# A two-layer spectral and feed-forward kernel: first stage rebuilt, folds moved to the vector engine, sums moved into matmuls, and a new instruction order

## The chip, the cores and the metric

The kernel runs on one core of a Trainium2 chip. The metric is device time in microseconds (us), the median of several executions. The engines are named as in the profile: PE (matmul), DVE (vector), ACT (scalar, here mostly copies out of PSUM), POOL (GpSimd), SP (issues DMAs).

## The reference, cut to what matters

```python
def _A_ref(x, w_r, w_i):                      # x: 1 x 2048 x 448
    X = rfft2(x) * (w_r + 1j * w_i)           # two-dimensional real FFT, pointwise filter
    return irfft2(X)
def _B_ref(x, w1, b1, w2, b2):                # 448 -> 1792 -> 448
    h = relu(x @ w1 + b1) ** 2
    return h @ w2 + b2
x = x + _A_ref(layernorm(x)); x = x + _B_ref(layernorm(x))
x = x + _A_ref(layernorm(x)); x = x + _B_ref(layernorm(x))
```

The Fourier transforms are matmuls with constant tables. A layer passes through these stages, and the text uses their names: **A** (first factor along the 2048 rows), **TD** (along the 448 columns), **B** (second factor along the rows), **W** (the filter, on DVE), **Bi, TI, AI** (the inverse of B, TD, A), then LayerNorm and the two dense matmuls. The stretch from TI to the first dense matmuls is called the ramp. A fold is the sum and the difference of two halves; a mirror is a row of the filter W read backwards. A row tile is 128 x 448, and there are 16.

## The kernel before

Instructions are recorded with their reads and writes, then a list scheduler fixes the order on every engine before anything runs. A unit with a higher `bias` goes first among those that are ready in the scheduler's model. At run time an engine takes its instructions in that order, as ACT does in the trace: its square root at 12.68 us (below) has its input from 10.04 us on, but stands behind an eviction, for which ACT waits idle for 0.47 us.

The first stage, per tile: DVE makes the statistics, ACT the square root, DVE the reciprocal and a 128 x 128 tile `Ms` of -2 x mean, POOL the scaled table `Fs`; PE runs five matmuls of 256 columns; ACT evicts.

```python
def first_A(t, evac):
    f, m = Fs[:, t % 4, :], Ms[:, t % 4, :]
    ts(f, FA_sb[:], rstd[:, t, 0:1], 1.0, ALU.mult, ALU.mult, eng="pool")
    ts(m, ones[:], mv[:, t, 0:1], -2.0, ALU.mult, ALU.mult)
    stage_A(t, x_sb[:, t, 0:D], xr[:, t, :], f, m, evac)
def w_direct():                               # six copies on POOL: rows of W to their places
    for a, b in ((0, 3), (3, 7)):
        cp(Wp[:, a:b, 0, 0:225], Wn[:, 0, a + 1:b + 1, :], eng="pool")
        ...
def w_mirror(p):                              # reversed rows of W by matmul, evicted by ACT
    ...
    act(Wp[:, p - 1, 1:4:2, 0:225], q[...])
def stage_W(p0, n):                           # the filter for the pairs p0 .. p0+n-1
    ...
    tt(T[6], T[3], T[2], ALU.subtract)
    tt(T[7], T[4], T[5], ALU.add)
    tt(z[:, :, 0], T[6][:, :, 1], T[6][:, :, 0], ALU.subtract)      # four folds
    tt(z[:, :, 3], T[6][:, :, 1], T[6][:, :, 0], ALU.add)
    tt(z[:, :, 1], T[7][:, :, 0], T[7][:, :, 1], ALU.subtract)
    tt(z[:, :, 2], T[7][:, :, 0], T[7][:, :, 1], ALU.add)
def second_A(t):                              # first stage of the second layer: 4 x 256 columns
    y = yA[:, t % 8, :]
    for h in range(2):
        ts(y[:, HD * h:HD * (h + 1)], x_sb[:, t, 0:HD] if h == 0 else x_sb[:, t, D - 1:HD - 1:-1],
           mv[:, t, 0:1], rstd[:, t, 0:1], ALU.subtract, ALU.mult)
    stage_A(t, y[:, 0:HD], y[:, HD:D], FA_sb[:], None, "act")
```

Of the kernel before, what the change touches and what calls it, by code (L numbers as in the profile page):

```python
# [19 lines left out]
EPS = 1e-5  # L20

# [9 lines left out]
def make_constants():  # L31
# [61 lines left out]
    return dict(FA=np.concatenate([FA, -FA], 1), FI=np.concatenate([FI, -FI], 1), TD=TD, G=G, H=H, TI=TI,  # L93
                J=np.eye(P)[::-1])


class _Op:
    __slots__ = ("eng", "fn", "deps", "has_dep", "ticket", "is_dma", "dsem", "cost", "lat", "unit", "gdeps")

    def __init__(self, eng, fn, is_dma, cost, lat):  # L100
        self.eng = eng
        self.fn = fn
        self.deps = []
        self.gdeps = []
        self.has_dep = False
        self.ticket = None
        self.is_dma = is_dma
        self.dsem = None
        self.cost = cost
        self.lat = lat  # L110
        self.unit = None

# [46 lines left out]
def _pages(ap):  # L159

    if isinstance(ap, _PsAP):
        return [ap.tile]
    pat = list(ap.ap)
    row = pat[0][0]
    name = ap.tensor.name
    off = np.array([ap.offset % row if row else ap.offset])
    for step, cnt in pat[1:]:
        off = (off[:, None] + step * np.arange(cnt)[None, :]).reshape(-1)
    pg = np.unique(off * mybir.dt.size(ap.dtype) // 8)
    return [(name, int(i)) for i in pg]  # L170


class _Sched:
# [6 lines left out]
    DMA_RATE = 280.0  # L180

    def __init__(self):
# [4 lines left out]
        self.bias = 0.0  # L187

# [39 lines left out]
    def schedule(self):  # L228
# [24 lines left out]
        free = {e: 0.0 for e in self.ENGINES}  # L253
        done = {}
# [4 lines left out]
        dma_free = 0.0  # L259
        for u in self.units:  # L260
            if left[u] == 0:
                cand[u.eng].append(u)
# [26 lines left out]
        while total:  # L289
            choice = None  # L290
            for e in self.ENGINES:
                best = None
                avail = {}
                for u in cand[e]:
# [7 lines left out]
                    start = max(r, free[e])  # L302
                    key = (start, -u.prio, u.seq)
                    if best is None or key < best[0]:
                        best = (key, u)
                if best is not None and (choice is None or best[0] < choice[0]):
                    choice = best
            assert choice is not None, "no unit can run"
            start, u = choice[0][0], choice[1]
            e = u.eng  # L310
            cand[e].remove(u)
# [12 lines left out]
            for op in u.ops:  # L324
# [3 lines left out]
                if op.is_dma:  # L328
                    dma_free = max(dma_free, t) + op.lat
                    done[op] = dma_free + 1800.0  # L330
                for a in (op.gdeps if e != "pe" else ()):
                    if a.eng == "pe" and a.unit.tile is not None:
                        for i in range(a.unit.tile.bank, a.unit.tile.bank + a.unit.tile.n):
                            bank_free[i] = max(bank_free[i], t + op.lat)
            free[e] = t
            for v in order[u]:
                left[v] -= 1
                if left[v] == 0:
                    cand[v.eng].append(v)
        self.length = max(done.values())  # L340
        for e in self.ENGINES:
# [33 lines left out]
def bass_interleave_layers__spectral_gfnet__dense_activation_squared_relu__prompt_kernel(nc, A_x, A_w_r, A_w_i, B_x, B_w1, B_b1, B_w2, B_b2, out):  # L375
# [6 lines left out]
    with ExitStack() as es:  # L382
# [7 lines left out]
        x_sb = sb("x_sb", [P, NT, 4 * P])  # L390
        XA = sb("XA", [P, 2, 2, 16, P])
# [12 lines left out]
        Wn = yT[:].rearrange("p a b c -> p (a b c)")[:, 0:2 * 16 * 225].rearrange("p (r k l) -> p r k l", r=2, k=16)  # L404
# [3 lines left out]
        H_sb = sb("H_sb", [P, 9, 2, 2 * P])  # L408
# [5 lines left out]
        Ms = sb("Ms", [P, 4, P])  # L414
# [3 lines left out]
        c_rem = sb("c_rem", [P, FF], FP32)  # L418
# [56 lines left out]

        def tt(o, a, b, op, eng="dve"):
# [19 lines left out]

        x_dram = A_x.rearrange("b (p t) d -> p (b t) d", t=NT)
# [7 lines left out]
        for a, b in pieces:  # L505
            dma("sp", x_sb[:, a:b, 0:D], x_dram[:, a:b, :])
        memset(ones[:], 1.0, eng="pool")
        memset(x_sb[:, :, D:4 * P], 0.0, eng="pool")
        memset(Wt[:, :, 224:226], 0.0, eng="pool")
        memset(W1_sb[64:128, 3, :], 0.0)  # L510
        for a, b in pieces:
            cp(xr[:, a:b, :], x_sb[:, a:b, D - 1:HD - 1:-1], eng="pool")

        for i, w in enumerate((A_w_r, A_w_i)):
            dma("sp", Wn[:, i, :, :], w.rearrange("(p k) l -> p k l", k=16))
        dma("sp", J_sb[:], dc["J"])
        dma("sp", G_sb[:, 2:9], dc["G"][:, 2:9])
        dma("sp", H_sb[:, 2:9], dc["H"][:, 2:9])
        dma("sp", G_sb[:, 0:2], dc["G"][:, 0:2])
        dma("sp", H_sb[:, 0:2], dc["H"][:, 0:2])  # L520
        dma("sp", TI_sb[:], dc["TI"])
# [6 lines left out]
        def w1_aux():  # L528

            qs = []  # L530
            for i in range(4):
# [6 lines left out]
                act(c_rem[64:97, f], q[lambda b: ps[64:97, b, 0:D]], ACT.Copy, scale=-1.0 / D)  # L538
            for r in (65, 67):
                dma("sp", W1_sb[r:r + 1, 3, :], B_b1.rearrange("(o f) -> o f", o=1))  # L540
            lo, c = W1_sb[96:97, 3, :], c_rem[96:97, :]
            tt(lo, c, lo, ALU.subtract)


        Wp = Wt[:, 0:28, :].rearrange("p (q s) l -> p q s l", s=4)
        W08 = Wt[:, 28:32, :].rearrange("p (q s) l -> p q s l", s=2)

        def w_direct():
            for a, b in ((0, 3), (3, 7)):
                cp(Wp[:, a:b, 0, 0:225], Wn[:, 0, a + 1:b + 1, :], eng="pool")  # L550
                cp(Wp[:, a:b, 2, 0:225], Wn[:, 1, a + 1:b + 1, :], eng="pool")
            for i in range(2):
                cp(W08[:, :, i, 0:225], Wn[:, i, 0:9:8, :], eng="pool")

        def w_mirror(p):

            q = _Tile(1)
            for i in range(2):
                mm(q[lambda b, i=i: ps[:, b, i * LW:i * LW + 225]], J_sb[:], Wn[:, 1 - i, 16 - p, :],
                   i == 0, i == 1, skip=True)  # L560
            act(Wp[:, p - 1, 1:4:2, 0:225],
                q[lambda b: ps[:, b, 0:2 * LW].rearrange("p (r l) -> p r l", r=2)[:, :, 0:225]])


        def ln_stats(ts_):
            for t in ts_:
                small(lambda e, t=t: e.bn_stats(st[:, t, 0:6], x_sb[:, t, 0:D]), [x_sb[:, t, 0:D]], [st[:, t, 0:6]], 540.0)  # L567
                small(lambda e, t=t: e.bn_aggr(mv[:, t, 0:2], st[:, t, 0:6]), [st[:, t, 0:6]], [mv[:, t, 0:2]])  # L568
            a, b = ts_[0], ts_[-1] + 1
            act(mv[:, a:b, 1], mv[:, a:b, 1], ACT.Sqrt, bias=epst[:, 0:1])  # L570

# [8 lines left out]
        def stage_A(t, y, yr, F, M, evac):  # L580
            q = _Tile(1)
            F2 = F[:, None, 0:P].to_broadcast([P, 2, P])
# [4 lines left out]
            for k in range(2):  # L587
                d0 = D0[k]
                mm(o(k), y[:, d0:d0 + P], F2, k == 0, False, skip=True)
                mm(o(k), yr[:, d0:d0 + P], F, False, k == 1 and M is None, skip=True)  # L590
            if M is not None:
                mm(q[lambda b: ps[:, b, :].rearrange("p (k g c) -> p k g c", k=2, g=2)[:, :, 0, :]], M, F2,
                   False, True, skip=True)
            src = q[lambda b: ps[:, b, :].rearrange("p (k c j) -> p k c j", k=4, c=16)]
            dst = XA[:, :, :, :, 8 * t:8 * t + 8].rearrange("p k g c j -> p (k g) c j")
            if evac == "act":
                act(dst, src)
            else:
                cp(dst, src)

        def first_A(t, evac):

            f, m = Fs[:, t % 4, :], Ms[:, t % 4, :]
            ts(f, FA_sb[:], rstd[:, t, 0:1], 1.0, ALU.mult, ALU.mult, eng="pool")
            ts(m, ones[:], mv[:, t, 0:1], -2.0, ALU.mult, ALU.mult)
            stage_A(t, x_sb[:, t, 0:D], xr[:, t, :], f, m, evac)


        def stage_TD(p):
            q = _Tile(2)  # L610
# [5 lines left out]
            act(U[:, 2 * p:2 * p + 2, :], q[lambda b: ps[:, b:b + 2, 0:2 * LW]])  # L616

        def stage_B(p):
            q = _Tile(2)
# [18 lines left out]
            act(EF[:, 2 * p:2 * p + 2, :], q[lambda b: ps[:, b:b + 2, 0:2 * LW]])  # L638

        def stage_W(p0, n):  # L640

            if p0 > 0:
# [10 lines left out]
                tt(T[5], T[1], wa, ALU.mult)  # L653
                tt(T[6], T[3], T[2], ALU.subtract)
                tt(T[7], T[4], T[5], ALU.add)
                z = Z[:, 4 * p0:4 * (p0 + n), :].rearrange("p (q s) l -> p q s l", s=4)
# [16 lines left out]
        def stage_Bi(p):  # L673
            q = [_Tile(1), _Tile(1)]
            if p > 0:
                i = p + 1
                z = Z[:, 4 * p:4 * p + 4, :]
                for lb in range(2):
                    for g in range(2):
# [3 lines left out]
                    act(VT[:, lb, :, :, 2 * p:2 * p + 2, :],  # L683
                        q[lb][lambda b: ps[:, b, :].rearrange("p (g t c j) -> p g t c j", g=2, t=16, c=2)])
            else:
                z = Z[:, 0:4, :].rearrange("p (q s) l -> p q s l", s=2)
                for lb in range(2):
# [4 lines left out]
                    for c in range(2):  # L692
                        act(VT[:, lb, :, :, c, :],
                            q[lb][lambda b, c=c: ps[:, b, c * 256:(c + 1) * 256].rearrange(
                                "p (g t j) -> p g t j", g=2, t=16)])


        def stage_TI(t, n):
# [6 lines left out]
            act(TIo[:, t:t + n, :, :], q[lambda b: ps[:, b:b + n, 0:D].rearrange("p i (g d) -> p i g d", g=2)])  # L705

        def stage_AI(t, n):
# [14 lines left out]
            for i in range(n):  # L722
                xx = x_sb[:, t + i, 0:D].rearrange("p (h d) -> p h d", h=2)
                r = q[lambda b, i=i: all_.f(b)[:, :, i, :]]
                small(lambda e, xx=xx, r=r, i=i: e.scalar_tensor_tensor(  # L725
                    out=xx, in0=_res(r), scalar=1.0, in1=xx, op0=ALU.mult, op1=ALU.add, accum_out=sd[:, t + i, 0:1]),
                    [r, xx], [xx, sd[:, t + i, 0:1]], 600.0)
# [3 lines left out]
        def ln_B(t, n):  # L731
# [17 lines left out]
            sch.bias -= 30000.0  # L749
# [3 lines left out]
            sch.bias += 30000.0  # L753
# [23 lines left out]
        def second_A(t):  # L777
            y = yA[:, t % 8, :]
            for h in range(2):
                ts(y[:, HD * h:HD * (h + 1)], x_sb[:, t, 0:HD] if h == 0 else x_sb[:, t, D - 1:HD - 1:-1],  # L780
                   mv[:, t, 0:1], rstd[:, t, 0:1], ALU.subtract, ALU.mult)
            stage_A(t, y[:, 0:HD], y[:, HD:D], FA_sb[:], None, "act")
# [3 lines left out]
        def spectral(first):  # L786
            items = (1, 2, 3, 4, 5, 6, 7, 0)
# [124 lines left out]
```

## Time and profile before

| | before |
|---|---|
| time, median | 311.0 us (309.89 to 311.18) |
| span of the profiled execution | 310.7 us |
| first TD matmul (end of the first stage) | 25.32 us |
| first TI matmul of layer 1 (end of the first spectral part) | 54.03 us |
| last tile's addition in layer 1 | 166.48 us |
| first TD of layer 2 | 170.44 us |
| first TI of layer 2 | 199.42 us |
| last tile's addition in layer 2 | 307.49 us |

The marks are starts of instructions in the timeline. The differences between them give stages that tile the span exactly. The page's first part has the busy time of each engine, its share of the span and the number of instructions:

```profile
PE 279.3 (90%) x1710; PEld 166.4 (54%) x1710; DVE 192.7 (62%) x606; ACT 181.8 (58%) x381; POOL 17.3 (6%) x34
```

Ninety per cent is an average over unlike stages. The view by windows shows one stage alone; its columns are the window, its length, busy us and instructions of PE, PEld, DVE, ACT and POOL, the granted clock, the DMA share and GB/s:

```profile
30.00:40.00 10.00, 9.23 (x78) 7.02 (x77) 9.86 (x27) 10.00 (x18) 0.00 (x0) 1.00 0.00 1
40.00:50.00 10.00, 8.67 (x58) 5.16 (x56) 9.72 (x22) 9.93 (x19) 0.00 (x0) 1.00 0.01 2
```

In the first spectral part DVE and ACT are both saturated, and PE waits for them. The first stage looks different. In PE's timeline (start, length, engine, line, operation, what was written from what, and in brackets the idle time before and what ended it):

```profile
7.72 0.37 PE L455 MATMUL ps<-Fs,x_sb 128*128 128x256 bf16 x1 [7.72 <-POOL Fs L487]
7.89 0.42 PE L455 MATMUL ps<-Fs,VT 128*128 128x256 bf16 x1
...
20.10 0.27 PE L455 MATMUL ps<-Fs,x_sb 128*128 128x256 bf16 x1
20.21 0.27 PE L455 MATMUL ps<-Fs,VT 128*128 128x256 bf16 x1
...
25.32 1.74 PE L455 MATMUL ps<-TD_sb,XA 128*128 128x226 bf16 x16 [0.88 <-ACT XA L474]
```

The lengths overlap (the first ends at 8.09 us, the second starts at 7.89), so the step from one start to the next is what counts. It is about 0.21 us for 256 columns at the beginning and 0.109 us after 19.9 us: half rate first, full rate later. Meanwhile ACT's timeline has a square root (`mv`) right behind evictions (`XA`) that wait for those slow matmuls,

```profile
12.18 0.60 ACT L474 ACTIVATE XA<-ps 128x512 bf16<-128x512 f32 x1 [0.47 <-PE ps L455]
12.68 0.29 ACT L474 ACTIVATE mv<-mv,epst 128x2 f32<-128x2 f32 x1
```

and DVE's timeline shows who waits for the square root:

```profile
9.96 0.59 DVE L567 BATCH_NORM_STATS2 st<-x_sb 128x6 f32<-128x448 bf16 x1
13.00 0.17 DVE L575 RECIPROCAL rstd<-mv 128x2 f32<-128x2 f32 x1 [2.45 <-ACT mv L474]
13.08 0.40 DVE L487 TENSOR_SCALAR Ms<-ones,mv 128x128 bf16<-128x128 bf16 x2
```

DVE, whose statistics every later step of the stage needs, stands idle for 2.45 us, because ACT's queue has the eviction first. The group of the `Ms` operations (count, then busy us in all, mean ns of one, idle us before them):

```profile
L487 DVE TENSOR_SCALAR Ms<-ones,mv 128x128 bf16<-128x128 bf16 x16 | 3.2, 242 | 0.0
```

And the end of layer 1 in PE's timeline:

```profile
162.76 1.04 PE L455 MATMUL ps<-FA_sb,tmp 128*128 128x256 bf16 x8
...
170.44 3.98 PE L455 MATMUL ps<-TD_sb,XA 128*128 128x226 bf16 x24 [0.69 <-ACT XA L474]
...
177.50 2.54 PE L455 MATMUL ps<-TD_sb,XA 128*128 128x226 bf16 x24 [0.25 <-ACT arena L474]
```

After a wait for the last tile 24 TD matmuls take 3.98 us at 170.44, and the next 24, seven us later, take 2.54 us: PE had dropped to half rate again.

### The profile page before, as it was taken

The numbers are of one execution on the slowest core, as the hardware profiler recorded it, in microseconds if no ns is written. First come the engines' busy times: TensorE is split into PE (matmuls) and PEld (weight loads), VectorE is DVE, ScalarE is ACT, GpSimd is POOL, SyncE is SP. The second block draws the span as 40 slices with busy tenths as digits, with TensorE's granted clock in tenths as the row PEclk, the third lists the DMA queues.
The fourth block names the chain that finished last, engine by engine and source line by source line (L and its number), as shares of the span: only waits on it lengthen the run. The fifth ranks groups of instructions, "written<-read, shape, count | busy, mean of one in ns | idle before, by whom it ended". The sixth has DMA issues, their size and how long they took to land.

```text
span 310.7 us, 4816 instructions
## 1 busy us (share of the span) xinstructions
PE 279.3 (90%) x1710; PEld 166.4 (54%) x1710; DVE 192.7 (62%) x606; ACT 181.8 (58%) x381; POOL 17.3 (6%) x34
## 2 busy tenths in 40 slices
PE   0798997989999999999996987787999999999995
PEld 0566664758554554555453664555854454454452
DVE  5661997898575476596465399498624443473431
ACT  2468999899246427735713688698804623651620
POOL 4655000000000000000000000000000000000000
PEclk9999999999999999999999899999999999999999
DMA  7997000074000000030000000016000020013001
GB/s 225 420 394 214 1 2 1 10 107 89 2 1 2 0 0 3 0 62 8 0 0 0 2 1 0 2 34 127 12 31 32 0 63 32 0 33 96 0 15 44
DMA packets 25435, 16.03 MB, mean 52 GB/s; under 512 B 17666, under 2 KB 24322, under 8 KB 25412
## 3 DMA queue, kind: packets, MB, share of 16 engines
q1 hardware_dynamic: 25124, 15.44, 17.8%
q10 hardware_dynamic: 288, 0.30, 0.3%
q8 instruction: 13, 0.21, 0.3%
q14 instruction: 10, 0.08, 0.1%
HBM read 9.70 MB, written 1.84 MB: 37 GB/s over the span
## 4 chain that ended last, share of the span: by engine, by line
PE 72%; ACT 11%; DVE 10%; issue 3%; DMA 1%; POOL 1%; SPq 0%; DVEq 0%; POOLq 0%
PE ps L455 72%; DVE tmp L478 5%; ACT arena L474 4%; ACT VT L474 3%; DVE x_sb L725 2%; DVE arena L478 2%; ACT sq_out L733 1%; DMA x_sb<-in_A_x_dram 1%; ACT XA L474 1%; ACT Wt L474 1%; DVE st L567 1%; POOL Fs L487 1%; DVE x_sb L773 0%; ACT sd L474 0%; ACT tmp L474 0%
## 5 line engine op out<-in xcount | busy, mean ns | idle before, releaser
L474 ACT ACTIVATE arena<-ps 128x512 bf16<-128x512 f32 (+2 forms) x172 | 99.0, 598 | 55.8 <-PE ps L455 53.8
L455 PE MATMUL ps<-yT,W_sb 128*128 128x512 bf16 (+1 forms) x560 | 99.7, 337 | 2.8 <-ACT arena L474 2.5
L455 PE MATMUL ps<-W_sb,arena 128*128 128x448 bf16 x448 | 87.0, 352 | 0.0
L455 PEld LDWEIGHTS ps<-yT,W_sb 128*128 128x128 bf16 x560 | 54.1, 98 | 46.3 <-ACT arena L474 4.4
L478 DVE TENSOR_TENSOR arena<-arena 128x512 bf16<-128x512 bf16 (+1 forms) x140 | 51.8, 372 | 42.4 <-ACT arena L474 37.3
L455 PEld LDWEIGHTS ps<-W_sb,arena 128*128 128x128 bf16 x448 | 43.7, 98 | 39.9 <-DVE x_sb L773 0.2
L773 DVE SCALAR_TENSOR_TENSOR x_sb<-ps,r,arena 128x448 bf16<-128x448 f32 x32 | 21.9, 683 | 33.4 <-PE ps L455 33.4
L474 ACT ACTIVATE XA<-ps 128x512 bf16<-128x512 f32 x32 | 18.4, 596 | 19.2 <-PE ps L455 19.2
L725 DVE SCALAR_TENSOR_TENSOR x_sb<-ps,x_sb 128x448 bf16<-128x448 f32 x32 | 19.1, 619 | 6.4 <-PE ps L455 6.3
L474 ACT ACTIVATE mv<-mv,epst 128x1 f32<-128x1 f32 (+1 forms) x24 | 7.0, 293 | 25.9 <-DVE mv L568 24.6
L733 ACT ACTIVATE sq_out<-x_sb 128x448 bf16<-128x448 bf16 x32 | 18.2, 570 | 5.1 <-DVE x_sb L725 4.8
L567 DVE BATCH_NORM_STATS2 st<-x_sb 128x6 f32<-128x448 bf16 x32 | 19.4, 616 | 2.8 <-DMA x_sb<-in_A_x_dram 2.3
L455 PE MATMUL ps<-H_sb,arena 128*128 128x256 bf16 x128 | 17.0, 273 | 3.9 <-DVE arena L478 2.4
L455 PE MATMUL ps<-Fs,x_sb 128*128 128x256 bf16 x32 | 11.2, 361 | 10.2 <-POOL Fs L487 10.2
L474 ACT ACTIVATE VT<-ps 128x512 bf16<-128x512 f32 (+1 forms) x36 | 17.2, 599 | 2.3 <-PE ps L455 2.3
L478 DVE TENSOR_TENSOR tmp<-arena 128x904 bf16<-128x904 bf16 (+1 forms) x16 | 8.4, 566 | 14.7 <-ACT arena L474 14.7
L455 PE MATMUL ps<-arena,G_sb 128*128 128x452 bf16 (+1 forms) x72 | 13.9, 333 | 3.6 <-ACT VT L474 3.0
L455 PE MATMUL ps<-TD_sb,XA 128*128 128x226 bf16 x128 | 15.4, 277 | 1.8 <-ACT XA L474 1.6
L455 PEld LDWEIGHTS ps<-H_sb,arena 128*128 128x128 bf16 x128 | 11.8, 98 | 8.6 <-DVE arena L478 6.3
L455 PE MATMUL ps<-TI_sb,VT 128*128 128x224 bf16 x128 | 14.6, 259 | 2.0 <-ACT VT L474 1.8
L474 ACT ACTIVATE tmp<-ps 128x896 bf16<-128x896 f32 (+1 forms) x18 | 14.7, 827 | 2.9 <-PE ps L455 2.9
L455 PE MATMUL ps<-tmp,FI_sb 128*128 128x448 bf16 (+1 forms) x72 | 14.7, 332 | 1.6 <-ACT tmp L474 1.5
(52 smaller groups left out, 219.9 us busy)
## 6 DMA issues: line engine op xcount, KB each, us to landing
out_dram<-x_sb SPq DMA_DIRECT2D x16, 112.0 KB, 1.7
W_sb<-in_B_w_dram SPq DMA_DIRECT2D x1, 1568.0 KB, 15.9
x_sb<-in_A_x_dram SPq DMA_DIRECT2D x3, 448.0 KB, 7.1
W_sb<-in_B_w_dram SPq DMA_DIRECT2D x1, 1344.0 KB, 15.6
yT<-in_A_w_r_dram SPq DMA_DIRECT2D x1, 900.0 KB, 10.1
yT<-in_A_w_i_dram SPq DMA_DIRECT2D x1, 900.0 KB, 11.4
H_sb<-c_H SPq DMA_DIRECT2D x1, 896.0 KB, 12.5
G_sb<-c_G SPq DMA_DIRECT2D x1, 672.0 KB, 8.9
```

The lines of the kernel that those rows point to most:

```text
L455: sch.add("pe", lambda e: e.matmul(_res(o), lhsT, rhs, start=start, stop=stop, skip_group_check=skip), [lhsT, rhs], [o], cost=max(_free(rh ...
L474: sch.add("act", lambda e: e.activation(o, _res(i), func, **kw), rd, [o], cost=c)
L478: sch.add(eng, lambda e: e.tensor_tensor(o, _res(a), b, op), [a, b], [o], cost=_free(o) / rate + 69.0)
L487: sch.add(eng, lambda e: e.tensor_scalar(o, i, s1, s2, op0=op0, **kw), rd, [o], cost=_free(o) * 0.83 + 245.0 if eng == "pool" else _free(o ...
L567: small(lambda e, t=t: e.bn_stats(st[:, t, 0:6], x_sb[:, t, 0:D]), [x_sb[:, t, 0:D]], [st[:, t, 0:6]], 540.0)
L725: small(lambda e, xx=xx, r=r, i=i: e.scalar_tensor_tensor(out=xx, in0=_res(r), scalar=1.0, in1=xx, op0=ALU.mult, op1=ALU.add, accum_out=sd ...
L733: sch.add("act", lambda e, i=i: e.activation(sq_out[:, i % 2, :], x_sb[:, i, 0:D], ACT.Square, accum_out=sd[:, i, 1:2]), [x_sb[:, i, 0:D]] ...
L773: small(lambda e: e.scalar_tensor_tensor(out=o, in0=_res(i), scalar=r2[:, t, 0:1], in1=xb[:, t, :], op0=ALU.mult, op1=ALU.add), [i, r2[:, ...
```

## The change

Its intent: let the first stage run at the pace of the statistics, take work off DVE and ACT in the spectral parts by giving PE a little more, and halve PE's work in the second layer's A stage. The diff, cut to its core:

```diff
+SD_PAIRS = (4, 5, 6, 7)
+HS = ...                                     # tables [-H1, H0, H1, -H0] of the four pairs, 1 MB
+PR = {'A1': 73200.0, 'A1step': 1700.0, 'TD': [-3800.0, -9200.0], 'B': [33100.0, 25400.0], ...}
 # scheduler: dummy matmuls into gaps of PE in the scheduler's model
+                while self.warm_fn is not None:
+                    gap = start - free["pe"]
+                    ...
+                    self.ops["pe"].append(d)
 # first stage
-            dma("sp", x_sb[:, a:b, 0:D], x_dram[:, a:b, :])
+            dma("sp", xin[:, a:b, :], x_dram[:, a:b, :])          # dense
-            ts(m, ones[:], mv[:, t, 0:1], -2.0, ALU.mult, ALU.mult)
+                ts(m2[:, a:b, 0], mv[:, a:b, 0], -2.0, 1.0, ALU.mult, ALU.mult)   # two tiles at once
+            mm(..., m2[:, t, 0:1].to_broadcast([P, P]), F2, False, True, skip=True)
-        w_direct()                                                # POOL copies; now DMAs place the rows
+            dma("sp", Wp[:, :, 2 * i, 0:225], w_dram[i][:, 1:8, :])
 # mirrors are evicted by DVE; the scheduler may give A evictions to ACT or DVE
-            act(Wp[:, p - 1, 1:4:2, 0:225], ...)
+            evac(Wp[:, p - 1, 1:4:2, 0:225], ..., EV["M"])        # EV["M"] = ['dve']
 # filter and Bi of the pairs 4 to 7: no folds, four matmuls of 512 columns for four of 256
+                if p0 in SD_PAIRS:
+                    tt(z[:, :, 0:2], T[3], T[2], ALU.subtract)
+                    tt(z[:, :, 2:4], T[4], T[5], ALU.add)
+                    return
+                        for n, f in enumerate((hs[:, 3:1:-1], hs[:, 1:3], hs[:, 2:0:-1], hs[:, 0:2])):
+                            mm(q[lb][...], z[:, n, L0[lb]:L0[lb] + P], f, n == 0, n == 3)
 # A stage of layer 2: fold on DVE, then 4 x 128 columns
+                        tt(E, a, b, ALU.add)
+                        tt(O, a, b, ALU.subtract)
+                        ts(E, E, mv[:, t, 2:3], rstd[:, t, 0:1], ALU.subtract, ALU.mult)
+                        ts(O, O, rstd[:, t, 0:1], 1.0, ALU.mult, ALU.mult)
 # order: every stage gets its own tuned bias
-                sch.bias = 3000.0 * (8 - n)
+                sch.bias = PR[k][L] - PR["step"][L] * n
-                sch.bias = 22000.0 * (5 - t // 4) - 500.0 * t
+                base = PR["ramp"][L] - PR["rstep"][L] * t if t < 4 else PR["late"][L] - PR["lstep"][L] * t
```

Also changed: the W1 column sums (w1_aux, 16 matmuls) no longer go through an fp32 copy `c_rem` on ACT; the TD and B stages of pair 2 go through tiles of one bank, whose evictions the scheduler may give to ACT or DVE (`SPLIT`); the scheduler's model of DMAs is new, and it tracks dependencies in pieces of 4 bytes, not 8.

## The prediction

It was written before the changed kernel was built or run. That gain was a term of the sum, so the sum is cut too. It came to about -15 us; the terms that stand, of the points 1, 2, 4 and 5, make -7 -3 -1.3 -1.5 = -12.8 us.

> **What bounds the kernel now.** The busy table has PE at 279.3 of 310.7 us. Stages, off the timeline (us from the span's start):
> - 0 to 25.3, first stage: 16 tiles of statistics, scaling, matmul. The first matmul starts at 7.72; up to 19.75 the 256-column matmuls follow every 0.213 us, afterwards every 0.109 us, so 41 of them run at half rate though the page's clock row shows 9s. PE waits 10.2 us on POOL's Fs (waits view). Square roots sit on ACT behind evictions that wait for slow matmuls (DVE idle 2.45 us at 10.5).
> - 25.3 to 54.0, first spectral part: ACT and DVE both 97 to 100% busy between 30 and 50 (windows view).
> - 54 to 67.8 inverse transform and LayerNorm (ramp); 67.8 to 166.3 dense matmuls.
> - 166.3 to 170.4: last tile's chain; PE cools: 24 TD matmuls take 3.98 us there, 2.54 later.
> - 170.4 to 199.4, second spectral part: bound by DVE's chain (176.3 to 198.1).
> - 199.4 to 215.9 ramp, dense matmuls to 307.5, 3 us of tail.
>
> By matmul cadence about 265 us of PE work are necessary; 46 us are idle or cold.
>
> **What changes, costed.**
> 1. First stage: 16 Ms scalings leave DVE (3.2 us), six W copies leave POOL (4.2 us), dummy matmuls warm PE before the first real one, evictions may go to DVE. Then statistics rule: 16 x about 0.63 us plus small operations, from 3.6 us, 12 to 13 us; then Fs, five matmuls, eviction. TD starts at about 18 instead of 25.3: -7 us.[...]
> 2. Spectral parts: mirror evictions leave ACT (7 x 0.44 us) for DVE, early, where DVE idles 7.4 us. c_rem leaves ACT (1.7 us). Four pairs drop the folds in SBUF: 8 x 0.30 = 2.4 us of DVE per part. PE pays: 8 matmuls of 512 columns for 8 of 256 in four pairs, 4 x 0.85 = 3.4 us per part. DVE falls, PE nearly becomes the limit: -1.5 us each part.
> 3. Second A: 4 x 128 columns for 4 x 256 per tile.[...] DVE pays about 0.55 us a tile, 9 us in all, hidden under dense matmuls except 0.3 us at the last tile.
> 4. Dummies keep PE warm over the last-tile gap: -1.3 us.
> 5. New priorities, two ramps: -1.5 us together. Half a megabyte more constants: no cost.
>
> [...]with w1_aux (3 us of PE) moved, about neutral.
>
> **Predicted time: 296 us; 290 to 302 eight times in ten.** Faster by over 2%: 0.93; within 2%: 0.06; slower: 0.01.
>
> **What would show it.** First-stage matmuls every 0.109 us from the first real one; first TD at 17 to 19 us; no POOL copies of Wt; mirror evictions on DVE before 30 us. Spectral parts of 26 to 28 us, Bi steps of 0.216 us.[...] TD after the dense part at full rate. Dense steps unchanged at 0.19 and 0.216 us.
>
> **What would make it wrong.** Dummies delaying real work; W rows in 450-byte pieces arriving late; evictions on DVE standing ahead of statistics; w1_aux landing just before the first layer's matmuls; the added PE work lengthening the spectral parts. If the ramps are reordered well, nearer 290.

## The result, and the profile after

The changed kernel takes 297.87 us (297.63 to 298.33); the kernel before took 311.09 us in the same rounds. The ratio is 0.9584, with a 95% interval of 0.9557 to 0.9612. Ratios here are the mean time of one kernel's fast runs over that of the other's fast runs of the same rounds, so not quite the ratio of the medians. Executions over 1.5% slower than the fastest of the same kernel are left out of the means.

By stages, in the profiled executions (spans 310.7 and 296.6 us):

| stage | before | after | difference |
|---|---|---|---|
| first stage, to the first TD | 25.32 | 20.61 | -4.71 |
| spectral part, layer 1, to the first TI | 28.71 | 26.74 | -1.97 |
| TI, AI, LayerNorm and dense, layer 1 | 112.45 | 109.59 | -2.86 |
| last tile to the first TD of layer 2 | 3.96 | 3.85 | -0.11 |
| spectral part, layer 2 | 28.98 | 26.34 | -2.64 |
| TI, AI, LayerNorm and dense, layer 2 | 108.07 | 106.51 | -1.56 |
| last addition to the end | 3.2 | 2.9 | -0.3 |

The profiled execution of the kernel before took 312.5 us, about 1.5 above the median, so the spans differ by more than the medians do.

The busy table of the kernel after; PE is busy for as long as before in a span 14 us shorter:

```profile
PE 281.0 (95%) x1728; PEld 163.9 (55%) x1730; DVE 197.3 (67%) x647; ACT 174.8 (59%) x367; POOL 12.6 (4%) x28
```

PE's timeline, first stage:

```profile
7.67 0.27 PE L516 MATMUL ps<-Fs,xin 128*128 128x256 bf16 x1 [1.38 <-POOL Fs L557]
7.78 0.27 PE L516 MATMUL ps<-Fs,VT 128*128 128x256 bf16 x1
...
20.61 2.53 PE L516 MATMUL ps<-TD_sb,XA 128*128 128x226 bf16 x24
```

Matmuls step by 0.109 us from the first one. TD comes at 20.61, not at 18. PE's timeline around the layer change:

```profile
144.91 0.61 PE L516 MATMUL ps<-FA_sb,tmp 128*128 128x128 bf16 x8
...
157.68 1.25 PE L960 MATMUL ps<-ones 128*128 128x512 bf16 x5 [0.45 <-DVE x_sb L874]
...
160.79 2.54 PE L516 MATMUL ps<-TD_sb,XA 128*128 128x226 bf16 x24 [0.69 <-ACT XA L540]
...
178.73 7.07 PE L516 MATMUL ps<-HS_sb,arena 128*128 128x512 bf16 x31
```

Five dummies (written from `ones`) fill the wait, and the 24 TD matmuls then take 2.54 us. The eight 128-column matmuls at 144.91 span 0.61 us; one lasts 0.22 us, so their step is (0.61 - 0.22) / 7 = 0.056 us. From 178.73 PE works through 31 recorded matmuls of 512 columns (one of the 32 is missing from the record). In the same stretch DVE has its last filter work at 183.52, then waits 5.49 us for PE:

```profile
183.52 0.69 DVE L548 TENSOR_TENSOR arena<-tmp 128x452 bf16<-128x452 bf16 x2
189.70 0.62 DVE L826 SCALAR_TENSOR_TENSOR x_sb<-ps,x_sb 128x448 bf16<-128x448 f32 x1 [5.49 <-PE ps L516]
```

So PE sets the end of this spectral part now. In layer 1's part, too, PE is busy for 26.25 of the 26.74 us (windows view), where it was busy for 25.67 of 28.71 before. Where the first stage lost its 2.6 us against the prediction is in the group that replaced `Ms`:

```profile
L557 DVE TENSOR_SCALAR m<-mv 128x2 bf16<-128x2 f32 x8 | 3.2, 403 | 0.1
```

Eight operations on two elements a partition take 3.2 us, exactly what the sixteen `Ms` operations of 128 elements took. DVE's timeline has the two longest,

```profile
9.86 0.81 DVE L557 TENSOR_SCALAR m<-mv 128x2 bf16<-128x2 f32 x1
...
14.25 0.76 DVE L557 TENSOR_SCALAR m<-mv 128x2 bf16<-128x2 f32 x1
```

and POOL's timeline has what runs meanwhile:

```profile
9.71 0.93 POOL L552 COPY VT<-xin 128x896 bf16<-128x896 bf16 x1
...
14.05 0.93 POOL L552 COPY VT<-xin 128x896 bf16<-128x896 bf16 x1
```

The first `m` ends at 9.86 + 0.81 = 10.67 us, the POOL copy at 10.64; the second at 15.01, the copy at 14.98. Six of the eight run beside a POOL operation; they take 0.33 to 0.81 us, and each ends 0.02 to 0.03 us after a POOL operation does. The two that meet no POOL operation take 0.17 and 0.15 us. In this trace, then, the operation seems to be held until POOL is done; why is not shown. Whether a reduction that makes the same number is held too is what the first experiment asks.

### The profile page after: what moved, and what is told of

It reads as the page before. It is cut to its first block, busy times and chain, and to the rows that moved or that the text cites. A ratio compares the mean times of both kernels' runs of the same rounds, so it can differ in the third digit from the quotient of the medians.

```text
span 296.6 us, 4902 instructions
## 1 busy us (share of the span) xinstructions
PE 281.0 (95%) x1728; PEld 163.9 (55%) x1730; DVE 197.3 (67%) x647; ACT 174.8 (59%) x367; POOL 12.6 (4%) x28
## 4 chain that ended last, share of the span: by engine, by line
PE 80%; DVE 9%; ACT 6%; issue 2%; DMA 1%; POOL 0%; SPq 0%; DVEq 0%
PE ps L516 80%; DVE tmp L548 3%; ACT VT L540 2%; DVE st L643 2%; DMA xin<-in_A_x_dram 1%; ACT sq_out L834 1%; ACT arena L540 1%; DVE arena L548 1%; ACT tmp L540 1%; DVE m L557 1%; DVE x_sb L826 1%; DVE x_sb L874 0%; DVE mv L644 0%; ACT sd L535 0%; DVE arena L541 0%
## 5 line engine op out<-in xcount | busy, mean ns | idle before, releaser
L516 PE MATMUL ps<-yT,W_sb 128*128 128x512 bf16 (+1 forms) x560 | 98.7, 336 | 1.3 <-DVE x_sb L826 0.9
L535 ACT ACTIVATE arena<-ps 128x512 bf16<-128x512 f32 (+1 forms) x140 | 70.4, 515 | 43.9 <-PE ps L516 41.6
L540 ACT ACTIVATE arena<-ps 128x904 bf16<-128x904 f32 (+1 forms) x32 | 26.1, 889 | 3.2 <-PE ps L516 3.1
L540 ACT ACTIVATE XA<-ps 128x512 bf16<-128x512 f32 x29 | 16.4, 592 | 17.0 <-PE ps L516 17.0
L548 DVE TENSOR_TENSOR tmp<-tmp,Wt 128x904 bf16<-128x904 bf16 (+1 forms) x32 | 16.0, 562 | 0.0
L516 PE MATMUL ps<-HS_sb,arena 128*128 128x512 bf16 x62 | 14.2, 379 | 0.1
L516 PE MATMUL ps<-TD_sb,XA 128*128 128x226 bf16 x128 | 13.6, 260 | 0.7 <-ACT XA L540 0.7
L516 PEld LDWEIGHTS ps<-TI_sb,VT 128*128 128x128 bf16 x128 | 12.1, 98 | 3.4 <-ACT VT L540 2.3
L516 PEld LDWEIGHTS ps<-TD_sb,XA 128*128 128x128 bf16 x128 | 12.2, 97 | 1.9 <-ACT XA L540 1.0
L826 DVE SCALAR_TENSOR_TENSOR x_sb<-ps,x_sb 128x448 bf16<-128x448 f32 x16 | 9.4, 622 | 5.6 <-PE ps L516 5.5
## 6 DMA issues: line engine op xcount, KB each, us to landing
W_sb<-in_B_w_dram SPq DMA_DIRECT2D x1, 1344.0 KB, 11.3
```

The source lines that it names most:

```text
L516: sch.add("pe", lambda e: e.matmul(_res(o), lhsT, rhs, start=start, stop=stop, skip_group_check=skip), [lhsT, rhs], [o], cost=max(_free(rh ...
L535: sch.add("act", lambda e: e.activation(o, _res(i), func, **kw), rd, [o], cost=c)
L540: op = sch.add(engs[0], lambda e: e.activation(o, _res(i), ACT.Copy) if h[0].eng == "act" else e.tensor_copy(o, _res(i)), [i], [o], cost=c ...
L548: sch.add(eng, lambda e: e.tensor_tensor(o, _res(a), b, op), [a, b], [o], cost=_free(o) / rate + 69.0)
L826: small(lambda e, xx=xx, xi=xi, r=r, i=i: e.scalar_tensor_tensor(out=xx, in0=_res(r), scalar=1.0, in1=xi, op0=ALU.mult, op1=ALU.add, accum ...
```

## The experiments

Ten kernels ran, all with correct results. Times are medians. Since the kernel before ran beside each of them (310.4 to 311.4 us), ratios compare across jobs best (three jobs, each on another chip); the kernel after has 0.9584.

One more reading helps with several of them. A trace has a record of the clock granted to PE, and the windows view gives its mean. From its first entry on, it reads full but for spells of 0.50, which last 3.41 us (in experiment 8 6.83 us). Apart from the last microseconds of a run, the profile of the kernel before has one spell, at the layer change (170.09 to 173.50), and that of the kernel after has none. The mean granted clock of every execution is on record as well: in the profiled ones it is 0.999 or 1.000 without a spell, 0.993 or 0.994 with one, and 0.989 with two or with the long one. In experiments 3, 5 and 9, executions of one kernel that are one such step apart differ by 0.7 to 1.8 us on the mean; it is not the only cause of spread (experiment 7 has 300.56 us at 1.000).

### 1. The mean by a reduction

```diff
-    ts(m2[:, a:b, 0], mv[:, a:b, 0], -2.0, 1.0, ALU.mult, ALU.mult)
+    tensor_reduce(m2[:, a:b, 0], mv[:, a:b, 0:1].to_broadcast([P, b - a, 2]), axis=X, op=ALU.add)
-    mm(..., m2[:, t, 0:1].to_broadcast([P, P]), F2, False, True)              # -2 mean x F
+    mm(..., m2[:, t, 0:1].to_broadcast([P, P]), <-F>, False, True)            # 2 mean x -F
```

> The kernel after, with one operation changed: the eight first-stage DVE operations that make twice the mean (2 elements a partition, 403 ns on the mean, up to 808 ns, several ending together with a POOL operation) are a reduction instead of a tensor_scalar; the order on every engine stays. Theory 1: the tensor_scalar is held by a running POOL operation[...], and it stands in the chain. Then the eight fall to under 0.2 us each whatever POOL does, the first TD comes at 18.3 to 19.5 us instead of 20.6, and the time falls by 1 to 2 us. Rival: the end of the first stage is set by PE and by ACT's evictions. Then the eight get shorter, but TD stays at 20.2 or later and the time moves by less than 0.5 us.

Measured: 296.3 us (296.14 to 296.43), ratio 0.9521 (0.9497 to 0.9544). The group became

```profile
L650 DVE TENSOR_REDUCE m<-mv 128x2 bf16<-128x4 f32 x8 | 1.2, 149 | 0.1
```

and one of them in DVE's timeline, with the POOL copy that runs through it:

```profile
9.57 0.15 DVE L650 TENSOR_REDUCE m<-mv 128x2 bf16<-128x4 f32 x1
```

```profile
9.43 0.93 POOL L552 COPY VT<-xin 128x896 bf16<-128x896 bf16 x1
```

It runs 0.15 us in the middle of a POOL copy. TD comes at 18.90 us, as PE's timeline has it:

```profile
18.90 1.35 PE L516 MATMUL ps<-TD_sb,XA 128*128 128x226 bf16 x12
```

From the first real matmul to TD it is 11.51 us against 12.94 (this takes out when the input landed: the first matmul came 0.28 us earlier). Theory 1 holds: the queue orders were the same on all engines, and only the kind of operation (with the sign of the table it goes with) differed. This version beats both kernels.

### 2. No dummies

```diff
-        sch.warm_fn = warm_mm
```

> The kernel after without its 20 dummy matmuls. Theory 1: half-rate matmuls set the first stage of before, and cool PE the start of the second spectral part. Then first-stage steps of 0.213 us return, TD comes 3 to 5 us later than 20.6, the second part's first 24 TD matmuls take about 4 us instead of 2.54, and the time rises by 4 to 6 us. Rival: DVE's statistics set the first stage and half-rate PE keeps up. Then TD moves by less than 1 us and the time rises by 1 to 2 us, all of it from the second part.

Measured: 299.87 us, ratio 0.964, so about 0.0056 x 311 = 1.7 us above the kernel after. PE's timeline, first stage (every line is one matmul of 256 columns until TD):

```profile
9.98 0.42 PE L516 MATMUL ps<-Fs,m 128*128 128x256 bf16 x1
10.20 0.35 PE L516 MATMUL ps<-Fs,xin 128*128 128x256 bf16 x1
10.39 0.27 PE L516 MATMUL ps<-Fs,VT 128*128 128x256 bf16 x1
10.50 0.27 PE L516 MATMUL ps<-Fs,xin 128*128 128x256 bf16 x1
...
20.44 0.76 PE L516 MATMUL ps<-TD_sb,XA 128*128 128x226 bf16 x6
```

Half rate lasts until 10.3 us, 15 or 16 matmuls, and TD comes at 20.44, no later than with dummies. From the first matmul to TD it is 13.40 us against 12.94. So here the dummies are worth half a microsecond. At the layer change:

```profile
159.20 0.53 PE L516 MATMUL ps<-FA_sb,tmp 128*128 128x128 bf16 x4 [2.34 <-DVE tmp L557]
160.41 4.16 PE L516 MATMUL ps<-TD_sb,XA 128*128 128x226 bf16 x24 [0.69 <-ACT XA L540]
...
166.80 2.53 PE L516 MATMUL ps<-TD_sb,XA 128*128 128x226 bf16 x24
```

The 24 TD matmuls take 4.16 us, the clock record has a half-rate spell from 160.54 to 163.95, and the second spectral part is 1.63 us longer. The rival was right for the first stage: in the new order, half-rate PE keeps up.

### 3. Second A stage without folds

```diff
-    mm(..., y[:, D0[k]:D0[k] + P], FA_sb[:, 0:P], ...)        # 4 x 128 columns, y = sums and differences
+    mm(o, y[:, D0[k]:D0[k] + P], F2, ...)                     # 4 x 256 columns, y as before
+    mm(o, y[:, HD + D0[k]:HD + D0[k] + P], FA_sb[:], ...)
-    tt(E, a, b, ALU.add); tt(O, a, b, ALU.subtract)
```

> The kernel after with the second A stage of before: four matmuls of 256 columns a tile, no folds on DVE. Theory 1: the dense stage is bound by PE alone and the 128-column matmuls step at 0.056 us, so 64 x 0.053 = 3.4 us come back in full; DVE's 9 us of folds buy no time when they leave. The time rises by 2.8 to 3.6 us.[...] Second rival: the folds lengthen the chain of the last tile, so taking them away gives something back and the rise stays under 1.5 us.

Measured: 304.87 us (303.12 to 306.1), ratio 0.9797: more than any theory said. By stages, layer 1's dense part is 113.01 us against 109.59, +3.4, close to what 64 x 0.053 us predicts (58 of the 64 matmuls lie in this stage, the others just behind it). Another 2.6 us lie in the second spectral part and 0.4 in the second dense part. PE's timeline at the layer change:

```profile
159.85 0.81 PE L957 MATMUL ps<-ones 128*128 128x512 bf16 x3
162.21 0.75 PE L516 MATMUL ps<-FA_sb,tmp 128*128 128x256 bf16 x4 [1.54 <-DVE tmp L557]
163.74 4.05 PE L516 MATMUL ps<-TD_sb,XA 128*128 128x226 bf16 x24 [0.78 <-ACT XA L540]
```

The scheduler's model saw a shorter gap and placed three dummies where the kernel after has five. PE was idle for 1.54 and 0.78 us behind them and dropped to half rate: 4.05 us for 24 TD matmuls. So about 3.4 us are the folds' worth. Of the 2.6 us in the second spectral part half rate accounts for some 1.6, as in experiment 2, a side effect of this edit through the dummies; the rest is not traced. The one execution with a granted clock of 1.000 took 303.12 us.

### 4. No sums on PE

```diff
-SD_PAIRS = (4, 5, 6, 7)
+SD_PAIRS = ()                                # HS is neither kept nor loaded
```

> The kernel after with no pair summed on PE: all seven pairs fold on DVE as before, the HS constants are not loaded. Theory 1, the prediction's: DVE bounds the spectral parts, so 2.4 us more on DVE cost about 1.5 us in each part, 3 us in all, although PE has 3.4 us less work in each. Rival: after the other changes PE is the limit of these parts (it is gapless from 176.9 to 186.7 us), and the sums only move the wait. Then the time is within 0.7 us of the kernel after, or less.

Measured: 302.57 us, ratio 0.9728. The spectral parts take 28.14 and 27.81 us against 26.74 and 26.34: +1.40 and +1.47, as theory 1 and the prediction have it. PE's timeline has the waits on DVE's folds (`DVE arena`) back:

```profile
179.15 0.28 PE L514 MATMUL ps<-H_sb,arena 128*128 128x256 bf16 x1 [1.11 <-DVE arena L546]
...
184.68 0.28 PE L514 MATMUL ps<-H_sb,arena 128*128 128x256 bf16 x1 [0.61 <-DVE arena L546]
...
199.98 1.65 PE L514 MATMUL ps<-tmp,FI_sb 128*128 128x448 bf16 x4 [2.15 <-ACT tmp L538]
```

The last line is something else: a wait of 2.15 us in the ramp of layer 2, where the kernel after has shorter ones (0.74 and 0.91 us). Behind it the clock record has a half-rate spell (199.67 to 203.08), and that stage is 2.03 us longer though nothing in its work changed; so the time rises by 4.5 us (0.0144 x 311), and not by the 3 us of theory 1. From the first TI of layer 2 on, ACT, DVE and PE run the same kinds of operation in the same order as in the kernel after, but for the dummies. Why the wait grew is not shown.

### 5. The old priorities

```diff
-                sch.bias = PR[k][L] - PR["step"][L] * n
+                sch.bias = 3000.0 * (8 - n)
 # and likewise for all stages: each bias as in the kernel before
```

> The kernel after with every priority of the list scheduler as before (the work is the same, only its order changes; the eight-times-larger set of tuned numbers is not used). Theory 1, the prediction's: the new order is worth about 1.5 us, in the ramps. By stages (marks: first TD, first TI, last tile's addition, each of both layers) the second dense stage goes back from 106.5 to about 108 us and the others move by less than 0.5 us each; the time rises by 1 to 2.5 us. Rival: the new order carries much more of the gain, in the first stage and in the spectral parts too. Then the time rises by 4 us or more.

Measured: 309.58 us (308.01 to 310.27), ratio 0.9948. The rival was right, and by far: with all of the new work, but in the old order, hardly anything is gained over the kernel before. Stages: 23.24, 27.90, 112.93, 3.95, 28.99, 107.86, 2.9 us. In layer 2's dense part there is a half-rate spell (208.06 to 211.48), which the kernel after has not.

### 6. The kernel before, with dummies

```diff
+        sch.ops["pe"][0:0] = dummies         # 12 matmuls of 512 columns ahead of PE's queue
```

> The kernel before with one thing added: 12 dummy matmuls of 512 columns at the front of the PE queue, about 5.2 us at half rate. Theory 1: in the kernel before, half-rate matmuls hold ACT's evictions, these hold the square roots behind them in ACT's queue, and so DVE and POOL; the kernel after gained little from its dummies only because its queue order no longer lets that happen. Then the first-stage steps are 0.109 us from the first one, DVE's wait of 2.45 us near 10.5 us goes, TD comes 2.5 to 4 us earlier than 25.3, and the time falls by as much. Rival: as in the kernel after, cold PE costs about half a microsecond here too, and the order of statistics and scalings sets the stage. Then TD comes less than 1 us earlier.

Measured: 309.71 us (307.92 to 310.21), ratio 0.9951. TD comes 3.4 us earlier,

```profile
21.90 1.73 PE L455 MATMUL ps<-TD_sb,XA 128*128 128x226 bf16 x16 [0.89 <-ACT XA L474]
```

and ACT's timeline shows the third square root at 10.79, where it was at 12.68:

```profile
8.65 2.23 ACT L474 ACTIVATE XA<-ps 128x512 bf16<-128x512 f32 x4 [0.69 <-PE ps L455]
10.79 0.29 ACT L474 ACTIVATE mv<-mv,epst 128x2 f32<-128x2 f32 x1
```

So in the old queue order the half-rate matmuls did hold the statistics, by way of ACT. The time fell by only about 1.5 us (0.0049 x 311), 2.3 us in the profiled execution, where the second spectral part is 0.6 us longer and the second dense part 0.3. The clock record shows what lengthened the spectral part. Besides the spell at the layer change it has another at the part's end, which the profile of the kernel before has not (windows view; the clock is the third number from the end):

```profile
193.33:196.74 3.41, 3.41 (x17) 2.11 (x15) 1.00 (x3) 2.65 (x6) 0.00 (x0) 0.50 0.00 0
```

The last 23 Bi matmuls before TI take 4.52 us there and 3.12 in the kernel before. Of the four executions, the two with the clock of two spells (0.988 and 0.989) took 310.08 and 310.21 us, the two with that of one (0.994) 309.34 and 307.92. Theory 1 is right about the stage, and half rate that came back later took a part of its gain away; the rest is not settled.

### 7. The reduction, and sums on PE for two pairs

```diff
-SD_PAIRS = (4, 5, 6, 7)
+SD_PAIRS = (6, 7)                            # on top of experiment 1
```

> The kernel of the first experiment (mean by a reduction) with sums on PE for pairs 6 and 7 only, not 4 to 7. Theory 1: each pair counts about the same, DVE bounds the parts throughout: half of the 1.4 us a part that the four pairs bring is lost, so the time is 1 to 2 us above the 296.3 us of the first experiment. Rival: with four pairs PE is already the limit at the end of a part, and two pairs do as well or better: within 0.5 us of 296.3, or below it.

Measured: 300.56 us (299.29 to 301.24), ratio 0.9659, some 4.3 us above experiment 1, where theory 1 had 1 to 2. The spectral parts are 0.79 and 1.21 us longer, so each pair counts, as theory 1 says. The rest lies in layer 2's dense part (+1.27 us in the profiled execution, without any change in its work, but the order on ACT, DVE and PE differs there) and in the spread of the executions.

### 8 to 10. Order and work taken apart

Experiment 8 is the kernel before with the new priorities:

```diff
+PR = {...}                                   # and every sch.bias as in the kernel after
```

> The kernel before with the new set of scheduler priorities and nothing else: the fourth corner of a square whose others are 310.9 us (old work, old order), 309.6 (new work, old order) and 297.9 (both new). Theory 1: the order has to fit the work, so the numbers help the old work little: 307 us or more, and the 13 us belong to the two together. Rival: the new order is good by itself (mirrors in DVE's idle time, fewer tiles before the dense stage), and the work's own share is what is left: 301 us or less.

Measured: 314.56 us, ratio 1.0136 (1.0097 to 1.0175): slower than the kernel before, though by less than 2%. By stages the loss lies in one: the first spectral part takes 33.84 us against 28.71. DVE's timeline shows two delays that the kernel before has not: a wait of 3.00 us for ACT, which has evicted all mirrors by 30.3 us (in the kernel before the last eviction starts at 39.48), and the column-sum operation on `c_rem`, ahead of the last filter operation:

```profile
34.52 1.17 DVE L481 TENSOR_TENSOR tmp<-arena 128x904 bf16<-128x904 bf16 x2 [3.00 <-ACT arena L477]
...
52.62 2.02 DVE L481 TENSOR_TENSOR W_sb<-c_rem,W_sb 1x1792 bf16<-1x1792 f32 x1
```

What each is worth was not tested. The long half-rate spell (52.04 to 58.87) begins there too. Elsewhere the new order helps the old work as well: the first stage is 2.4 us shorter, and layer 2's spectral and dense parts are 1.1 and 1.0.

| median, us | old order | new order |
|---|---|---|
| old work | 310.44 to 311.42 | 314.56 |
| new work | 309.58 | 297.87 |

The new work alone gains 0.5%, the new order alone loses 1.4%, both gain 4.2%. Experiments 9 and 10 split the order. Experiment 9 keeps the new priorities in the first stage, the spectral parts and w1_aux:

```diff
-                base = PR["ramp"][L] - ... ; sch.bias = PR["h"][L] + 22000.0 * (4 - c) - 500.0 * t0
+                base = 22000.0 * (5 - t // 4) - 500.0 * t ; sch.bias = 22000.0 * (4 - c) - 500.0 * t0
```

> The kernel after with new priorities in the first stage, the spectral parts and the w1 row sums, old ones in the ramps and dense stages. In the run with all old priorities the first stage lost 2.6 us, the spectral parts 1.2 and 2.7, the ramps with their dense stages 3.3 and 1.4. Theory 1: the stages add up, so this run gets back the first three and w1's share of the fourth: 301 to 303 us. Rival: the place where w1's row sums and the inverse transforms fall depends on both sets, and a mixed set is as bad as the old: 306 us or more.

Measured: 300.59 us (299.75 to 301.86), ratio 0.9678. Experiment 10 keeps them in the ramps and dense stages:

```diff
-                sch.bias = PR[k][L] - PR["step"][L] * n      # also A1, M, aux
+                sch.bias = 3000.0 * (8 - n)
```

> The complement: new priorities in the ramps and dense stages, old ones in the first stage, the spectral parts and the w1 row sums. Theory 1 (stages add up): 304 to 306 us, with the first TD near 23.2 us, spectral parts of about 28 and 29 us and dense stages near 109.6 and 106.5 us. Rival: 308 us or more, or 300 or less.

Measured: 306.0 us, ratio 0.9849, with the first TD at 23.58 and spectral parts of 27.88 and 27.82 us. Against the kernel after, experiment 9 loses 0.0094 x 311 = 2.9 us and experiment 10 loses 8.2, together 11.1; experiment 5, which undoes both, loses 11.3. In the total the two halves of the order add up, by stages they do not: layer 1's dense part is 1.9 us longer in experiment 9, 2.7 in experiment 10 (which had expected 109.6 us and got 112.25) and 3.3 in experiment 5. Two of the four executions of experiment 9, the profiled one among them, have the clock of one spell (in the profile 163.28 to 166.70, at the layer change); the two without took 299.75 and 299.92 us. One mechanism can be read in DVE's timeline of experiment 10, first stage:

```profile
15.34 2.21 DVE L541 CAST Wt<-ps 128x450 bf16<-128x450 f32 x4
17.47 0.15 DVE L655 RECIPROCAL rstd<-mv 128x2 f32<-128x2 f32 x1
```

Four evictions of mirrored W rows stand ahead of a reciprocal in DVE's queue, and in POOL's timeline the scaling waits for it:

```profile
17.71 0.93 POOL L557 TENSOR_SCALAR Fs<-FA_sb,rstd 128x256 bf16<-128x256 bf16 x2 [2.85 <-DVE rstd L655]
```

The prediction had named this danger ("evictions on DVE standing ahead of statistics"). So moving the mirrors to DVE costs time where the order does not keep them behind the statistics, as the priorities of the kernel after do for six of the seven.

## Why the prediction was right, point by point

The predicted time, 296 us with 290 to 302, holds the measured 297.87. The sum was about -15 us; the medians fell by 13.2 and the spans by 14.1. Its terms did not all measure what they were said to, and their errors partly cancelled, which is luck.

- **First stage, -7: too large; -4.71 was measured.** The term that was mis-sized is "16 Ms scalings leave DVE (3.2 us)". What replaced them cost the same 3.2 us: six of the eight small tensor_scalars ended only with a POOL operation and took 0.33 to 0.81 us. Experiment 1 removes that wait and TD comes at 18.90: 1.4 of the missing 2.6 us, and 0.3 by earlier input. The last 0.9 us are not accounted for.
- **The cause given for the first stage was incomplete.** Half-rate PE did hold the kernel before (experiment 6: TD at 21.90). But the new queue order removes the same wait without dummies (experiment 2: 20.44), so the two remedies do not add: dummies are worth 0.5 us there in the new order. The POOL copies of W, counted among the gains, were off the chain: in the kernel before they run from 23.56 us, behind the last scaling.
- **Spectral parts, -1.5 each: about right.** Both parts fell in the range of 26 to 28 us, by 1.97 and by 2.64 us; the second number includes the warm PE below, so that about 1.0 is left. Experiment 4 gives 1.40 and 1.47 us for the sums on PE alone. PE did become the limit at the end of the part.
- **Second A stage: its gain, an estimate that no run had shown, was too small.** The step was 0.056 us, against 0.109 for 256 columns, and the stage is worth about 3.4 us (experiment 3). The folds on DVE (0.26 and 0.24 us for the last tile) stay hidden, as predicted; the tail of the last tile did not grow (3.85 against 3.96 us).
- **Warm PE at the layer change, -1.3: right.** Without dummies the part is 1.63 us longer (experiment 2: 24 TD matmuls in 4.16 us, 2.54 with them).
- **Priorities, -1.5 in the ramps: about right in size, but not in place, and the weakest step.** Experiment 9 takes the new priorities out of the ramps and dense stages alone. Its executions without a half-rate spell are 2 us slower; layer 1's dense part grows by 1.9 us and layer 2's not at all (106.47 us). So the 1.56 us by which layer 2's dense part fell are not shown to come from these priorities. Undoing the priorities everywhere costs 11.3 us, and 8.2 of them go with the first stage, the spectral parts and w1_aux (experiment 10), for which the prediction has no such term: its other terms held only because the order was fitted to the new work. It named one such danger, evictions ahead of statistics, and gave it no price.

The errors had opposite signs: the first stage fell short by 2.3 us, the second A stage gave more than was expected of it. Open remain a part of what experiment 6 loses of its 3.4 us, and why each half of the old order costs time in layer 1's dense part, where together they cost 3.3 us.

## What to carry to other kernels

Cost a small operation by what it takes in the trace, not by its size: here a tensor_scalar on two elements took up to 0.81 us beside POOL and the reduction in its place 0.15, so where a small DVE operation ends together with POOL's, try another form of it. When queues are filled ahead of time, work moved to another engine can need an order made for it, so try the two apart and together before giving a gain to either, and look stage by stage: a new order that loses in all may lose in one stage alone. Dummy matmuls were cheap here (five took 1.25 us of a wait and kept the rate; the three of experiment 3, 0.81 us, did not), but their count must match the real gap, and an edit elsewhere can change that gap. Before explaining a stage that changed without a change in its work, look whether its clock did.

## What the traces show of PE's rate, and of DVE beside POOL

- A tensor_scalar on two elements a partition took up to 808 ns beside POOL operations, the reduction in its place 149 ns on the mean (experiment 1).
- The step of the 128-column matmuls was 56 ns with a new weight load for each, in runs of four and eight (the kernel after, from 144.91 us on).
- PE fell to half rate after gaps of 2.34 and 0.69 us with half a microsecond of work between (experiment 2), and after 1.54 and 0.78 us (experiment 3). It stayed at full rate with gaps of 0.45, 0.65 and 0.69 us and five dummies between (the kernel after). What goes with the fall in the clock records is PE's busy time in the 3.41 us before: 0.66 us in experiment 2 (157.12 to 160.54), 0.95 in the kernel before (166.68 to 170.09) and 1.48 in experiment 3 (161.05 to 164.47), after which the rate fell; 2.33 and 2.72 in the kernel after (156.26 to 163.09), where it stayed. With the traces of the kernels before and after cut into stretches of 3.41 us at the clock's switches, the least after which the rate stayed full is 1.71 us (6.07 to 9.48, the kernel after). That is read off these traces; no experiment set it.
- In the kernel before the clock switches at 19.90 and 170.09 us, 150.19 us apart, which is 44 times the length of a spell (3.41 us). The first matmul is at 7.72, and full rate came at 19.90. PE was busy for 2.48 us from 9.66 to 13.07 and for 2.56 us from there to 16.49, with the pause from 12.15 to 13.93 us in both, and for all 3.41 us to 19.90. In experiment 2 half rate lasted from the first matmul at 7.04 to about 10.3 us, by the steps.
- The clock record of a profile can begin late. In the kernel before its first entry is at 19.90 us; the windows view counts what is before as full and reads 1.00 from 0 to 20 us, with steps of 0.21 us.
